# Moving the denominator sums of two token tiles by one FFN group in a fused attention and FFN kernel

## The chip, the cores and the metric

The kernel runs on one core of one Trainium2 chip. The metric is device time in microseconds (us) of one execution. The time given for a kernel is the median of several executions. The profile shows one further execution, taken by the hardware profiler.

In this text PE is the matrix engine, PEld its weight loads, DVE the vector engine, ACT the scalar engine, POOL the GpSimd engine, and SP the engine that issues nearly all transfers of this kernel. Every engine works through its own instructions in the order in which they were written.

## The reference

The input has 2048 tokens of 512 features in bf16. Two branches are computed from the same `A_x` rows and mixed by a gate for each token. (Branch B is called with `x`, the rows of branch A.)

```python
qkv = x @ wqkv                       # 32 heads of 16 features
phi = lambda t: where(t > 0, t + 1, exp(t)) + 1e-6
pq, pk = phi(q), phi(k)
kv  = einsum("bhsd,bhse->bhde", pk, v)
z   = einsum("bhsd->bhd", pk)
num = einsum("bhqd,bhde->bhqe", pq, kv)
den = einsum("bhqd,bhd->bhq", pq, z)[..., None] + 1e-6
a   = merge_heads(num / den) @ wo

b   = (silu(x @ w1) * (x @ w3)) @ w2  # hidden width 1376
g   = sigmoid((x * gate_w).sum(-1))
out = g * a + (1 - g) * b
```

## The kernel before

The 2048 tokens are 16 tiles of 128 tokens, and 4 blocks of 4 tiles. The hidden width of 1376 is ten groups of 128 and a remainder of 96 features. The schedule is written out by hand: the order of the calls in the source is the order in each engine's queue, and an engine that waits holds up all that is queued behind it.

The first stage, to about 47 us, projects q and k for all tiles, applies `phi`, and sums the products of keys and tokens in four PSUM banks. Then come the four blocks. In each, `glu_step(tb, fc)` is called for the ten groups (fc = 0 to 9): four matmuls for the gate (line 264), four for the up projection (line 270), a Silu on ACT (line 275) and a product on DVE (line 276) that writes one slice of `hT`. After the groups, `out_step(tb, tt)` is called for the four tiles: four matmuls of the attention branch (line 430, which read `pqT` and `M2`), a scaling on ACT (line 435), eleven matmuls of the second FFN layer (line 443, ten over the groups and one over the remainder), the mix on DVE (line 447), and the store (line 460).

Two helpers stand between these steps.

`den_step(t)` makes the scaled queries of tile t. `den_sums` does three instructions on DVE: a sum over the 16 features of each head (line 287), an addition of 1e-6 (line 290), and a reciprocal (line 294). `den_products(t + 1)` then puts one product on POOL for the next tile (line 283, tile `pr`), and `den_scale(t)` one scaling on POOL (line 298, tile `pqs`) and one transposing transfer on SP's queue (line 303, into `pqT`). The POOL queue therefore holds the product of tile t + 1 ahead of the scaling of tile t.

`rem_step(tb)` computes the remainder of the hidden width and the gates of a block: two times eight matmuls into two banks (line 231), Silu and Tanh on ACT (lines 237 and 238), a product on DVE for each half (line 241, into `hrem`), two small DVE instructions that finish the gates (lines 246 and 250), and one transposing transfer on SP's queue (line 254, from `hrem` into the last slice of `hT`).

The banks are handed out in turn. `mm_tile` gives banks 4 to 7 one after the other; gate, up and both remainder halves each take one:

```python
def mm_tile():
    turn["mm"] += 1
    return bank[4 + (turn["mm"] - 1) % 4]
```

In block 0 the turn falls so: the eighth group (fc = 7) takes banks 5 and 6, the two remainder halves take banks 7 and 4, the ninth group (fc = 8) takes 5 and 6, and the tenth (fc = 9) takes 7 and 4. The first matmul of the tenth group waits for the DVE instruction of line 241 that empties bank 7, its fifth for the one that empties bank 4. (In the profile's view of instructions these four banks are called bank_144 to bank_147.)

In block 0 the order of the helpers is fixed by a table, `den_at`, and by the place of the calls inside the loop. Under the same fc the denominator step stands ahead of the remainder step. For blocks 1 to 3 both are called between the `out_step`s of the block before.

Of the kernel before, what the change touches and what calls it, by code (L numbers as in the profile page):

```python
# [16 lines left out]
def kernel(  # L17
# [363 lines left out]
    def z_step():  # L381
        zT = work.tile([P, KC], FP32, tag="zT", bufs=1, name="zT")
        nc.vector.tensor_reduce(out=zT[:], in_=zaT[:], op=ALU.add, axis=AX.X)
        nc.vector.tensor_copy(out=zTb[:], in_=zT[:])
        dq.dma_start(out=zrow[0, :].rearrange("(p kc) -> p kc", kc=KC), in_=zTb[:])
        dq.dma_start(out=zpk[:], in_=zrow[0:1, :].to_broadcast([P, D]))
# [73 lines left out]
            dq.dma_start(out=rows[:, cs], in_=o[:, cs])  # L460

    z_step()
    den_at = {5: 0, 6: 1, 7: 2, 8: 3}
    for tb in range(NTB):
        for fc in range(FC):
            glu_step(tb, fc)
# [49 lines left out]
```

## Time and profile before

| | before |
|---|---|
| median of 3 runs | 181.23 us (181.0 to 181.37) |
| profiled execution: time, span | 180.97 us, 179.3 us |
| PE busy | 173.4 us, 97% of the span |
| DVE busy | 101.7 us, 57% |
| ACT busy | 62.6 us, 35% |
| POOL busy | 62.8 us, 35% |
| granted PE clock | 1.0 throughout |

The profiled execution's own time is 1.67 us above its span, which is what lies around the instructions that the profile shows. The chain of work that ended last is followed backwards from the last instruction. Each step goes to what released it, or to the instruction before it on the same engine. PE carries 93% of that chain and DVE 4%. A matmul instruction overlaps the next one, so the distance between the starts of two rows says how fast PE advances, and not the length of a row.

### The profile page before, as it was taken

How to read it: one execution, taken by the hardware profiler on the slowest of the kernel's cores; microseconds unless marked ns; L12 is line 12 of the kernel's file. 1: busy time of each engine (PE TensorE's matmuls, PEld its weight loads, DVE VectorE, ACT ScalarE, POOL GpSimd, SP SyncE). 2: the span in 40 equal slices, each digit the busy share in tenths (PEclk: the TensorE clock that was granted, in tenths of full speed). 3: DMA queues.
4: the chain of work that ended last, by engine and by line, in shares of the span. 5: the costliest groups of instructions: out<-in, count | busy, mean ns of one | idle time of the engine just before them, and what ended most of it. 6: DMA issues, size and time to landing. Idle time of an engine off the chain costs nothing.

```text
span 179.3 us, 2489 instructions
## 1 busy us (share of the span) xinstructions
PE 173.4 (97%) x863; PEld 84.1 (47%) x879; DVE 101.7 (57%) x196; ACT 62.6 (35%) x114; POOL 62.8 (35%) x104
## 2 busy tenths in 40 slices
PE   8999999999999979999999999999999999999993
PEld 5444444444454544644444454444445544444452
DVE  1299789888775896566343256644335564333222
ACT  3354543544736332222323222232321323332130
POOL 5077657656300877445400044540004432000000
PEclk9999999999999999999999999999999999999999
DMA  5988959992103022233200003420000332000011
GB/s 171 269 206 238 168 103 331 386 349 80 33 0 29 0 59 59 62 88 88 59 0 4 0 29 88 91 59 4 0 0 29 88 91 59 0 0 0 29 37 54
DMA packets 29724, 15.41 MB, mean 86 GB/s; under 512 B 21552, under 2 KB 28048, under 8 KB 29712
## 3 DMA queue, kind: packets, MB, share of 16 engines
q1 hardware_dynamic: 29440, 15.25, 33.8%
q8 instruction: 7, 0.11, 0.3%
q10 hardware_dynamic: 272, 0.01, 0.1%
q14 instruction: 5, 0.04, 0.1%
HBM read 8.56 MB, written 2.10 MB: 59 GB/s over the span
## 4 chain that ended last, share of the span: by engine, by line
PE 93%; DVE 4%; issue 1%; DVEq 0%
PE bank L443 21%; PE bank L264 18%; PE bank L270 17%; PE bank L169 16%; PE bank L217 8%; PE bank L430 8%; PE bank L231 2%; PE bank L317 2%; DVE den L290 1%; DVE hT L276 1%; DVE den L287 1%; PE bank L405 0%; PE bank L418 0%; PE bank L323 0%; DVE o L447 0%
## 5 line engine op out<-in xcount | busy, mean ns | idle before, releaser
L276 DVE TENSOR_TENSOR hT<-bank,sg 128x512 bf16<-128x512 f32 x40 | 27.2, 681 | 31.6 <-PE bank L270 28.5
L264 PE MATMUL bank<-xT,w 128*128 128x512 bf16 x158 | 40.9, 379 | 1.4 <-DVE hrem L241 1.2
L443 PE MATMUL bank<-w,hT 128*128 128x512 bf16 (+4 forms) x197 | 40.6, 355 | 0.1
L275 ACT ACTIVATE sg<-bank 128x512 bf16<-128x512 f32 x40 | 23.9, 597 | 47.6 <-PE bank L264 46.5
L270 PE MATMUL bank<-xT,w 128*128 128x512 bf16 x154 | 40.3, 379 | 0.2
L298 POOL TENSOR_TENSOR pqs<-pq,rden 128x512 bf16<-128x512 bf16 x16 | 16.9, 1055 | 56.1 <-issue 50.8
L169 PE MATMUL bank<-wqk,xT 128*128 128x512 bf16 x126 | 30.8, 386 | 0.1
L447 DVE SCALAR_TENSOR_TENSOR o<-bank,omg_all,aga 128x512 bf16<-128x512 f32 (+2 forms) x18 | 12.4, 692 | 27.5 <-PE bank L443 27.4
L443 PEld LDWEIGHTS <-hT 128*128 128x128 bf16 (+1 forms) x198 | 18.5, 98 | 20.0 <-DMA hT<-hrem 0.2
L201 POOL TENSOR_TENSOR zacc<-zacc,pk 128x128 f32<-128x128 f32 x56 | 23.3, 445 | 10.4 <-DVE pk L187 10.4
L264 PEld LDWEIGHTS <-w 128*128 128x128 bf16 x160 | 15.6, 98 | 19.7 <-issue 1.4
L270 PEld LDWEIGHTS <-w 128*128 128x128 bf16 x160 | 15.7, 98 | 18.9
L283 POOL TENSOR_TENSOR pr<-pq,zb 128x512 f32<-128x512 bf16 x16 | 18.4, 1153 | 11.7 <-ACT zb L389 11.7
L435 ACT ACTIVATE aga<-bank,g_all 128x512 f32<-128x512 f32 x16 | 11.0, 687 | 28.9 <-PE bank L430 27.8
L169 PEld LDWEIGHTS <-xT 128*128 128x128 bf16 x128 | 12.6, 99 | 15.1 <-issue 0.5
L217 PE MATMUL bank<-pk,xN 128*128 128x512 bf16 x62 | 16.3, 379 | 0.2
L430 PE MATMUL bank<-M,pqT 128*128 128x512 bf16 x61 | 16.3, 378 | 0.2
L182 ACT ACTIVATE eq<-bank 128x512 bf16<-128x512 f32 x16 | 9.4, 597 | 16.0 <-PE bank L169 14.9
L187 DVE SCALAR_TENSOR_TENSOR pk<-bank,emk 128x512 bf16<-128x512 f32 x16 | 11.1, 692 | 1.6
L182 ACT ACTIVATE ek<-bank 128x512 bf16<-128x512 f32 x16 | 9.4, 597 | 7.1 <-PE bank L169 7.1
L187 DVE SCALAR_TENSOR_TENSOR pq<-bank,emq 128x512 bf16<-128x512 f32 x16 | 11.1, 692 | 0.6
L287 DVE TENSOR_REDUCE den<-pr 128x32 f32<-128x512 f32 x16 | 10.8, 676 | 0.0
(49 smaller groups left out, 82.9 us busy)
## 6 DMA issues: line engine op xcount, KB each, us to landing
w<-in_B_w_dram SPq DMA_DIRECT2D x3, 1280.0 KB, 10.6
out_dram<-o SPq DMA_DIRECT2D x15, 128.0 KB, 1.9
wqk<-in_A_wqkv_dram SPq DMA_DIRECT2D x4, 256.0 KB, 4.0
xN<-in_A_x_dram SPq DMA_DIRECT2D x1, 1024.0 KB, 5.8
xN<-in_A_x_dram SPq DMA_DIRECT2D x2, 256.0 KB, 3.0
xN<-in_A_x_dram SPq DMA_DIRECT2D x1, 512.0 KB, 3.7
wv<-in_A_wqkv_dram SPq DMA_DIRECT2D x1, 512.0 KB, 11.6
wo<-in_A_wo_dram SPq DMA_DIRECT2D x1, 512.0 KB, 12.5
```

What stands on the lines that cost most here:

```text
L169: nc.tensor.matmul(ps[:], lhsT=xT[:, kc, t * P : (t + 1) * P], rhs=w[:, kc, :], start=(kc == 0), stop=(kc == KC - 1),)
L182: nc.scalar.activation(out=e[:], in_=ps[:], func=ACT.Exp)
L187: nc.vector.scalar_tensor_tensor(out=dst, in0=ps[:], scalar=0.0, in1=em[:], op0=ALU.max, op1=ALU.add)
L201: nc.gpsimd.tensor_tensor(out=(zaccb if t == NT - 1 else zacc)[:, cs], in0=zacc[:, cs], in1=pk[t][:, cs], op=ALU.add,)
L217: nc.tensor.matmul(bank[kc][:], lhsT=xN[:, t, kc * P : (kc + 1) * P], rhs=pk[t][:], start=(t == 0), stop=(t == NT - 1),)
L264: nc.tensor.matmul(g_ps[:], lhsT=w1[:, kc, fs], rhs=xT[:, kc, tok], start=(kc == 0), stop=(kc == KC - 1),)
L270: nc.tensor.matmul(u_ps[:], lhsT=w3[:, kc, fs], rhs=xT[:, kc, tok], start=(kc == 0), stop=(kc == KC - 1),)
L275: nc.scalar.activation(out=sg[:], in_=g_ps[:], func=ACT.Silu)
L276: nc.vector.tensor_tensor(out=hT[tb][:, fc, :], in0=u_ps[:], in1=sg[:], op=ALU.mult)
L283: nc.gpsimd.tensor_tensor(out=pr[t][:], in0=pq[:, t, :], in1=zb[:], op=ALU.mult)
L430: nc.tensor.matmul(a_ps[:], lhsT=pqT[:, c, ts], rhs=M2[:, c, :], start=(c == 0), stop=(c == KC - 1),)
L443: nc.tensor.matmul(b_ps[:, 0:w], lhsT=hT[tb][:n, fc, tl], rhs=w2[:n, fc, cs], start=(fc == 0), stop=(fc == FC),)
```

## The change

In block 0 the denominator steps of the third and fourth tile (tiles 2 and 3) are called one group later each. Nothing else in the source changes.

```diff
     z_step()
-    den_at = {5: 0, 6: 1, 7: 2, 8: 3}
+    den_at = {5: 0, 6: 1, 8: 2, 9: 3}
     for tb in range(NTB):
         for fc in range(FC):
             glu_step(tb, fc)
             if tb == 0:
                 if fc in den_at:
                     den_step(den_at[fc])
...
                 if fc == 7:
                     rem_step(0)
```

The orders on PE, ACT and POOL are the same in both kernels. On DVE the three sums of tile 2 go from ahead of the two products of line 241 to behind the `hT` product of the ninth group; the three sums of tile 3 go from ahead of the `hT` product of the tenth group to behind it, ahead of the first line 447. On SP the transfer of line 254 and the line 303 transfer of tile 2 change places.

## The prediction

> **What bounds the kernel now.** I read the page's busy shares first (PE 97%), then the list of waits, to see what the other 3% holds. It has only one wait of PE for another engine after the start:
>
> ```profile
> PE bank L264 <- DVE hrem L241: 1.2, 1, 1.2
> ```
>
> The columns are engine, tile and line, what it waited for, total us, times, longest. The timeline of PE around that wait gives its place (start, us, engine, line; idle time in brackets):
>
> ```profile
> 63.63 1.03 PE L264 MATMUL bank<-xT,w 128*128 128x512 bf16 x3
> 64.50 1.03 PE L270 MATMUL bank<-xT,w 128*128 128x512 bf16 x4
> 66.68 1.02 PE L264 MATMUL bank<-xT,w 128*128 128x512 bf16 x4 [1.16 <-DVE hrem L241]
> 67.54 1.03 PE L270 MATMUL bank<-xT,w 128*128 128x512 bf16 x4
> 68.40 1.03 PE L430 MATMUL bank<-M,pqT 128*128 128x512 bf16 x4
> 69.27 2.54 PE L443 MATMUL bank<-w,hT 128*128 128x512 bf16 x11
> ```
>
> These are the ninth group, the tenth, and the start of the first out_step. Groups of four matmuls start 0.86 to 0.87 us apart when nothing waits. The tenth group should have started at 64.50 + 0.87 = 65.37 and started at 66.68, so the stop costs 1.31 us of PE's pace (the 1.16 in brackets is measured from the modelled end).
>
> The timeline of DVE in the same stretch says why line 241 came late:
>
> ```profile
> 63.66 0.63 DVE L276 TENSOR_TENSOR hT<-bank,sg 128x512 bf16<-128x512 f32 x1
> 64.21 0.67 DVE L287 TENSOR_REDUCE den<-pr 128x32 f32<-128x512 f32 x1
> 64.92 1.11 DVE L290 TENSOR_SCALAR den<-den 128x32 f32<-128x32 f32 x1
> 66.06 0.35 DVE L294 RECIPROCAL rden<-den 128x32 f32<-128x32 f32 x1
> 66.33 0.56 DVE L241 TENSOR_TENSOR hrem<-bank,sgr 128x192 bf16<-128x192 f32 x2
> 66.81 0.77 DVE L246 TENSOR_SCALAR g_all<-th_all 128x4 f32<-128x4 f32 x1
> 67.49 0.16 DVE L250 TENSOR_SCALAR omg_all<-th_all 128x4 f32<-128x4 f32 x1
> 67.56 0.68 DVE L276 TENSOR_TENSOR hT<-bank,sg 128x512 bf16<-128x512 f32 x1
> ```
>
> The three sums of tile 2 (64.21 to 66.33) stand ahead of line 241. One of them, the small addition of line 290, took 1.11 us where its median is 0.18. The timeline of POOL shows its company:
>
> ```profile
> 63.83 1.05 POOL L298 TENSOR_TENSOR pqs<-pq,rden 128x512 bf16<-128x512 bf16 x1 [0.51 <-DVE rden L294]
> 64.84 1.15 POOL L283 TENSOR_TENSOR pr<-pq,zb 128x512 f32<-128x512 bf16 x1
> 66.50 1.05 POOL L298 TENSOR_TENSOR pqs<-pq,rden 128x512 bf16<-128x512 bf16 x1 [0.51 <-DVE rden L294]
> 67.51 1.15 POOL L283 TENSOR_TENSOR pr<-pq,zb 128x512 f32<-128x512 bf16 x1
> ```
>
> Line 290 ends at 66.03, POOL's product at 65.99; line 246 (0.77 instead of 0.16) ends at 67.58, POOL's scaling at 67.55. Small additions on DVE end when the POOL instruction beside them ends. The chain that ended last runs over PE from 66.68 to the last mix at 176.33, with no wait for another engine. So 1.31 us taken from this stop should shorten the whole, if nothing else becomes late.
>
> **Part 1: line 241 no longer behind the sums of tile 2.** With those gone from its front, the first line 241 starts at 64.21, where the reduction started. Its inputs are there: ACT's Silu and Tanh of the halves end by 63.56 and 64.23. Before, PE restarted 0.35 us after the first line 241 began (66.33 to 66.68); now bank 7 is free for PE at 64.56, 0.81 us ahead of need. The second starts about 0.24 later and ends by about 64.8; bank 4 is needed at 65.37 + 0.86 = 66.23. PE therefore does not stop: minus 1.31 us. Could line 241 itself be held by POOL, which scales tile 1 from 63.83 to 64.88 and then makes a product to 65.99? Before, the second line 241 ran from about 66.57 with POOL busy from 66.50, and both were over in 0.56, so by the nearest row no. The other end is that it waits until 65.99: PE restarts at 66.34 and the gain is 66.68 - 66.34 = 0.34. I take the first, as it is the same instruction beside the same POOL work.
>
> **Part 2: lines 246 and 250.** They come up at 64.69 (two line 241s took 0.48 to the next start). By the row at 66.81, line 246 ends with the running POOL instruction although POOL has the next one ready: about 64.91, then line 250, DVE free about 65.0. The ninth group's hT product cannot start before PE ends at 65.53 plus the usual 0.11 (86.32 to 86.43 in block 1): 65.64. If line 246 is instead held through POOL's next product, it ends near 66.03 and the product starts at 66.17. Either way that product, at 67.56 before, is earlier.
>
> The Trainium skill, "SBUF — State Buffer", section "Who interferes with whom", says that a tensor_scalar may use the port pair that DVE shares with GpSimd, and that whoever issues first holds it for the whole instruction. It speaks against this change in so far as the blocked addition does not vanish but moves. On its words alone line 246 might lose again to the next POOL instruction; then the later end above holds, and the total is still the same. The long lines 290 and 246 agree with it.
>
> **Part 3: the sums of tile 2 behind the ninth hT product.** hT 65.64 to 66.33; reduction from about 66.25; line 290 at 66.96 with POOL idle (its product for tile 3 ended at 65.99, its scaling of tile 2 waits for these sums), so 0.18; reciprocal at 67.18 to 67.53. The tenth hT product is next at 67.45; PE finishes its operand at 66.23 + 1.03 = 67.26, so the sums hold it up by only 0.1. It ends at 68.08, or 68.6 with part 2's later end. The second-layer matmuls of the first out_step start at 67.96 (69.27 less 1.31) and advance 0.216 each (2.38 for eleven), so they reach the tenth slice at 69.90. Spare: 1.8, at worst 1.3. Cost nothing; beyond that spare each us costs one.
>
> **Part 4: the sums of tile 3 behind the tenth hT product.** Reduction at 68.00; line 290 at 68.71. POOL's scaling of tile 2 starts at 67.61 (0.08 after the reciprocal, as at 63.83) and the product of tile 4 runs about 68.62 to 69.77, so line 290 pays the long price of 1.11 here: +0.93 on what it was. The reciprocal ends at 70.20. Behind it waits the first mix (line 447), which PE releases at 67.96 + 2.54 = 70.50 plus 0.11. Hidden, with 0.4 to spare; and its bank is wanted again only at the third out_step's line 443, near 75.8. Line 290 of tile 4 then comes at 71.99 while POOL works until 72.44 and may lose 0.3; the next mix is not released before 73.85.
>
> **Part 5: POOL and SP.** POOL's order stands. The scaling of tile 2 goes from 66.50 to 67.61, that of tile 3 from 69.57 to 70.28. Each issues one transpose on SP (1.19 on the queue, 2.4 to landing). Line 254 now stands ahead of tile 2's transpose: its data is complete at 64.8, the transpose of tile 1 holds SP from 64.91 to 66.10, so it issues at 66.1 and lands at 68.5; the remainder's matmul needs it at 67.96 + 10 x 0.216 = 70.12. Before it was issued at 68.86 and the weight load waited 0.24 for it, hidden. Tile 2's transpose issues at 68.7, lands 71.1, and is needed by the third out_step at 76.22 - 1.31 = 74.9; tile 3's lands near 73.8 and is needed near 78.2. Tile 0's, unmoved, lands at 62.24 + 2.4 = 64.6 and is now needed at 67.10. The first store is issued after tile 3's transpose, 71.36 + 1.19 = 72.6, as before (72.70). All cost nothing.
>
> **The sum.** 180.97 - 1.31 = 179.66 for the profiled execution. That execution was 0.26 below the median of the runs; on the median, 181.23 - 1.31 = 179.92. I predict 179.9. Such a kernel's measurement can tell about 0.2%, or 0.36 us, from no change.
>
> **The rivals.** *Line 241 blocked by POOL*, or DVE otherwise late by 1.2 to 1.5 us: the gain shrinks to 0.34 and the time is 180.9, which counts as no change. Against it stands the unblocked line 241 at 66.33; for it, that POOL works there without a gap to 65.99. Chance 0.06. *The stop was not line 241's*, and the tenth group waits for something else that frees at 66.6: 181.2. Against it: DVE's next instructions in time are those of line 241, and PE starts 0.35 after the first. Chance 0.03. *Slower: tile 2's transpose becomes the wait.* It is issued 68.7 instead of 67.58 and wanted 1.31 earlier. If it landed after 10.4 us, as the large weight loads did, it would arrive at 79.1, PE would wait 79.1 - 74.9 = 4.2, and the time would be 179.9 + 4.2 = 184.1. It decides from a landing at 74.9, and the whole is slower by 0.2% from 74.9 + 1.31 + 0.36 = 76.6. Against it: the neighbouring transposes landed in 2.4 each. Chance 0.04. A lesser PE wait of some tenths inside the first out_steps, from part 3 or 4, is the rest of my doubt about the size, not the sign.
>
> **The numbers.** Full removal 0.87 (faster). The run spread (-0.23, +0.14 about the median), a new wait of up to 0.6 and the pace's last 0.05 give 179.5 to 180.5. Part of it stays at 180.9 or 181.2 in 0.09, slower in 0.04. Faster by over 0.2%: 0.88, with a little of the first rival; same 0.08; slower 0.04.
>
> **What would show it.** In the changed profile: no idle PE before the tenth group's line 264, which starts near 65.4; line 241 near 64.2; line 290 of tile 2 at 0.18 and of tile 3 near 1.1; line 254 issued near 66.1; the last mix near 175.0 and a span near 178.0. It would be wrong if line 241 stretched beside POOL, or if a wait of line 430 or 443 for pqT or hT appeared.

## The result, and the profile after

The changed kernel takes 179.75 us (median of 7 runs, 179.1 to 180.43), against 181.0 for the kernel before in 7 runs. The ratio is 0.9921, with a 95% interval of 0.9895 to 0.9946: 1.4 us less, between 1.0 and 1.9 (the two medians differ by 1.25). Its profiled execution took 179.95 us, with a span of 178.2.

The waits of PE in the profile after are down to one line, which lies at the program's start. The wait for line 241 is gone.

```profile
PE bank L317 <- PEq L500: 0.8, 1, 0.8
```

The timeline of PE after, the same groups as shown of before (start, us, engine, line):

```profile
64.78 1.03 PE L270 MATMUL bank<-xT,w 128*128 128x512 bf16 x4
65.64 1.03 PE L264 MATMUL bank<-xT,w 128*128 128x512 bf16 x4
66.50 1.03 PE L270 MATMUL bank<-xT,w 128*128 128x512 bf16 x4
67.37 1.03 PE L430 MATMUL bank<-M,pqT 128*128 128x512 bf16 x4
68.23 2.54 PE L443 MATMUL bank<-w,hT 128*128 128x512 bf16 x11
```

The tenth group's line 264 starts 0.86 after the line 270 ahead of it, where it was 2.18 before. No row has a bracket with idle time. This profile runs 0.28 later than the one before on reaching the ninth group (64.78 against 64.50), which has nothing to do with the change: the first transposes (line 323) and projections (line 169) at the program's start took longer, and the lag is 0.27 already where line 169 starts at 10.53 against 10.26. So I measure each profile from the start of the ninth group's line 270 to the start of the last mix (line 447). Before, that is 176.33 - 64.50 = 111.83; after, 175.30 - 64.78 = 110.52. The difference is 1.31.

The timeline of DVE after:

```profile
64.48 0.61 DVE L241 TENSOR_TENSOR hrem<-bank,sgr 128x192 bf16<-128x192 f32 x2
65.01 0.17 DVE L246 TENSOR_SCALAR g_all<-th_all 128x4 f32<-128x4 f32 x1
65.09 0.16 DVE L250 TENSOR_SCALAR omg_all<-th_all 128x4 f32<-128x4 f32 x1
65.91 0.69 DVE L276 TENSOR_TENSOR hT<-bank,sg 128x512 bf16<-128x512 f32 x1 [0.66 <-PE bank L270]
66.52 0.68 DVE L287 TENSOR_REDUCE den<-pr 128x32 f32<-128x512 f32 x1
67.23 0.18 DVE L290 TENSOR_SCALAR den<-den 128x32 f32<-128x32 f32 x1
67.44 0.35 DVE L294 RECIPROCAL rden<-den 128x32 f32<-128x32 f32 x1
67.72 0.63 DVE L276 TENSOR_TENSOR hT<-bank,sg 128x512 bf16<-128x512 f32 x1
68.26 0.67 DVE L287 TENSOR_REDUCE den<-pr 128x32 f32<-128x512 f32 x1
68.97 1.11 DVE L290 TENSOR_SCALAR den<-den 128x32 f32<-128x32 f32 x1
70.12 0.35 DVE L294 RECIPROCAL rden<-den 128x32 f32<-128x32 f32 x1
70.89 0.75 DVE L447 SCALAR_TENSOR_TENSOR o<-bank,omg_all,aga 128x512 bf16<-128x512 f32 x1 [0.42 <-PE bank L443]
```

Line 241 starts 2.13 earlier (64.48 - 0.28 = 64.20 against 66.33), line 290 of tile 2 takes its short 0.18, and the long 1.11 has moved to tile 3. After it and the reciprocal DVE still waits 0.42 for the first mix. The timeline of POOL after shows why the two trade lengths: POOL idles 1.61 ahead of the scaling of tile 2, through line 290 of that tile, and the product at 68.89 starts just ahead of line 290 of tile 3.

```profile
64.10 1.05 POOL L298 TENSOR_TENSOR pqs<-pq,rden 128x512 bf16<-128x512 bf16 x1 [0.51 <-DVE rden L294]
65.11 1.15 POOL L283 TENSOR_TENSOR pr<-pq,zb 128x512 f32<-128x512 bf16 x1
67.88 1.05 POOL L298 TENSOR_TENSOR pqs<-pq,rden 128x512 bf16<-128x512 bf16 x1 [1.61 <-DVE rden L294]
68.89 1.15 POOL L283 TENSOR_TENSOR pr<-pq,zb 128x512 f32<-128x512 bf16 x1
```

### The profile page after: what moved, and what is told of

Its sections match the earlier page's. It is cut to its first block, busy times and chain, and to the rows that moved or that the text cites. A ratio compares the mean times of both kernels' runs of the same rounds, so it can differ in the third digit from the quotient of the medians.

```text
span 178.2 us, 2489 instructions
## 1 busy us (share of the span) xinstructions
PE 173.6 (97%) x863; PEld 84.2 (47%) x879; DVE 101.6 (57%) x196; ACT 62.6 (35%) x114; POOL 62.8 (35%) x104
## 4 chain that ended last, share of the span: by engine, by line
PE 97%; issue 1%; DVE 0%
PE bank L443 21%; PE bank L264 20%; PE bank L270 19%; PE bank L169 16%; PE bank L217 8%; PE bank L430 8%; PE bank L231 3%; PE bank L317 2%; PE bank L323 1%; PE bank L405 1%; PE bank L418 0%; DVE o L447 0%
## 5 line engine op out<-in xcount | busy, mean ns | idle before, releaser
L201 POOL TENSOR_TENSOR zacc<-zacc,pk 128x128 f32<-128x128 f32 x56 | 23.3, 445 | 10.4 <-DVE pk L187 10.4
```

The costliest lines, as they stand in the source:

```text
L201: nc.gpsimd.tensor_tensor(out=(zaccb if t == NT - 1 else zacc)[:, cs], in0=zacc[:, cs], in1=pk[t][:, cs], op=ALU.add,)
```

## The experiments

The theory: PE stops because line 241 stands behind the sums of tile 2 on DVE, and those are long because line 290 waits for POOL. Its rivals: the sums of tile 3 carry part of the gain; the bank alone holds PE; DVE is simply too full there; line 290 is long for its own reasons. All kernels start from the kernel before. The stage is the stretch from the ninth group's line 270 to the last mix, worked out as above from the one profile that there is of each kernel. The times of whole runs are compared with runs of the kernel before on the same chip, and carry the scatter of the start: the ninth group's line 270 began anywhere from 63.89 to 64.93 in the profiles of this study. The profiled executions of the three kernels with a stage of 110.52 show it: they took 179.33, 179.58 and 179.95 us with that line at 64.16, 64.42 and 64.78.

| kernel | stage, us | against before | ratio of times, 95% interval |
|---|---|---|---|
| before | 111.83 | | |
| the change | 110.52 | -1.31 | 0.9921 (0.9895 to 0.9946) |
| remainder step first | 110.52 | -1.31 | 0.9924 (0.9902 to 0.9947) |
| tile 3 only | 111.83 | 0.00 | 1.0007 (0.9987 to 1.0027) |
| no addition for tile 2 | 111.22 | -0.61 | 0.9986 (0.9971 to 1.0001) |
| own banks | 111.76 | -0.07 | 0.9999 (0.9979 to 1.0018) |
| own banks, transfer first | 110.67 | -1.16 | 0.9932 (0.9911 to 0.9954) |
| both ahead | 113.86 | +2.03 | 1.0125 (1.0089 to 1.0162) |
| both behind the ninth | 110.52 | -1.31 | 0.9909 (0.9888 to 0.993) |
| both in the out stage | 111.80 | -0.03 | 0.9996 (0.9981 to 1.0011) |
| POOL scales first | 110.90 | -0.93 | 0.9953 (0.9935 to 0.997) |

**Remainder step first.** Tile 3 and the table stay; two calls trade places.

```diff
             if tb == 0:
+                if fc == 7:
+                    rem_step(0)
                 if fc in den_at:
                     den_step(den_at[fc])
...
-                if fc == 7:
-                    rem_step(0)
```

> Table of before; only the remainder step is called ahead of the denominator step of tile 2, within the same group, so on DVE line 241 passes the sums of tile 2, and on SP line 254 passes tile 2's transpose; tile 3 stays where it was. Theory (PE stops because line 241 stands behind the sums of tile 2): no stop of PE at the tenth group, 1.3 us less than before, 179.6 to 179.9. Rival (the gain needs the sums of tile 3 moved too, or the later place of the sums): the tenth hT product comes late and PE waits at the tenth slice; by my count this product ends at 69.65 and is wanted at 69.90, so a wait of a few tenths at most and 180.0 to 180.3.

The timeline of PE at the tenth group:

```profile
64.42 1.03 PE L270 MATMUL bank<-xT,w 128*128 128x512 bf16 x4
65.28 1.03 PE L264 MATMUL bank<-xT,w 128*128 128x512 bf16 x4
```

The whole 1.31 is there, with tile 3 unmoved. The tenth hT product starts at 68.92 and ends at 69.55 in this profile, and no row of PE shows a wait at the tenth slice. The two starts lie 0.86 apart: PE does not stop ahead of the tenth group. So it is enough that the remainder step goes ahead of tile 2's sums, on DVE and on SP. The additions of line 290 still wait for POOL there (0.43 for tile 2, 1.11 for tile 3), and it costs nothing.

**Tile 3 only.**

```diff
-    den_at = {5: 0, 6: 1, 7: 2, 8: 3}
+    den_at = {5: 0, 6: 1, 7: 2, 9: 3}
```

> Only the sums of tile 3 are moved behind the tenth group; tile 2 as before. Theory: the stop of 1.2 us at line 264 stays, the time is that of before, 181.0. Rival (the sums of tile 3, between the ninth and tenth hT products, cost something by themselves): 180.0 to 180.7.

The stage is that of before to 0.01, and the list of waits has the stop again:

```profile
PE bank L264 <- DVE hrem L241: 1.2, 1, 1.2
```

By itself, the half of the change that moves tile 3 is worth nothing.

**No addition for tile 2.**

```diff
-        nc.vector.tensor_scalar(
-            out=den[:], in0=den[:], scalar1=1e-6, scalar2=None, op0=ALU.add
-        )
+        if t != 2:
+            nc.vector.tensor_scalar(
+                out=den[:], in0=den[:], scalar1=1e-6, scalar2=None, op0=ALU.add)
```

> Order of before; the addition of 1e-6 (line 290) is left out for tile 2 only, which takes out the one instruction that ended with POOL's product at 66.0. Theory: line 241 starts at 65.2 instead of 66.3, PE's stop at the tenth group shrinks from 1.3 to about 0.2; but line 254 still stands behind tile 2's transpose on SP, which issues at 67.0, so the remainder slice of hT lands near 70.8 where PE wants it at 70.3: a new wait of about 0.5. Sum: 0.6 us less than before, 180.4. If line 254 is no limit: 1.1 less, 179.9. Rival (the length of line 290 is not POOL's doing and the next instruction takes it over): no change, 181.0.

The timeline of PE shows both parts of the sum, the small stop that is left and the new one:

```profile
64.15 1.03 PE L270 MATMUL bank<-xT,w 128*128 128x512 bf16 x4
65.19 1.02 PE L264 MATMUL bank<-xT,w 128*128 128x512 bf16 x4
...
67.78 2.32 PE L443 MATMUL bank<-w,hT 128*128 128x512 bf16 x10
70.45 0.39 PE L443 MATMUL bank<-w,hT 96*128 96x512 bf16 x1 [0.36 <-DMA hT<-hrem]
```

The tenth group starts 0.17 late (65.19 against 64.15 + 0.87), and the remainder's matmul 0.51 late (70.45 against 67.78 + 10 x 0.216). Together 0.68 of the 1.31 stay, and the stage gives 0.61. The runs' times show only 0.25 less, between 0.5 less and nothing; the 0.6 expected lies just outside, and I cannot say from these runs what makes up the rest.

**Own banks.** The remainder halves of block 0 take two banks that lie idle there.

```diff
-            ps = mm_tile()[:].rearrange("p (j n) -> p j n", j=2)
+            ps = (ab_tile if tb == 0 else mm_tile)()[:].rearrange("p (j n) -> p j n", j=2)
```

> Order of before on DVE, POOL and SP; the remainder step of block 0 takes two banks of the other turn, which lie idle there, so the tenth group no longer waits for line 241. Theory: PE does not stop at the tenth group, but line 241 and with it line 254 are as late as before (issue near 68.9), so the first out_step stops before its last matmul, for the remainder slice, until 71.4: the 1.3 us come back as a wait of PE for that transfer, and the time is 180.9 to 181.1. Rival (the bank is the whole cost): 179.7. It tells whether the bank alone, or the bank and the transfer behind the sums, held PE.

The bank's wait is gone and the time is not. The list of waits has a new one of PE in its place:

```profile
PE bank L443 <- DMA hT<-hrem: 0.9, 1, 0.9
```

The timeline of PE gives its place:

```profile
68.39 2.48 PE L443 MATMUL bank<-w,hT 128*128 128x512 bf16 x10
71.78 0.39 PE L443 MATMUL bank<-w,hT 96*128 96x512 bf16 x1 [0.91 <-DMA hT<-hrem]
```

PE came to the first out_step without a stop and then stood before the last of its matmuls, 71.78 against 68.39 + 2.16 = 70.55. The sums of tile 2 held PE by two ways: the bank, and the remainder's transfer. The second stood just behind the first; in the profile before it shows only as the 0.24 for which the weight load waited.

**Own banks, transfer first.** As above, and on SP line 254 passes tile 2's transpose; DVE's order is that of before.

```diff
-        dq.dma_start(out=pqT[:, :, t * P : (t + 1) * P], in_=pqs[:], transpose=True)
+        if t == 2:
+            held.append(pqs)
+        else:
+            dq.dma_start(out=pqT[:, :, t * P : (t + 1) * P], in_=pqs[:], transpose=True)
...
                 if fc == 7:
                     rem_step(0)
+                    dq.dma_start(out=pqT[:, :, 2 * P : 3 * P], in_=held[0][:], transpose=True)
```

> As the kernel with own banks for the remainder halves of block 0, and on SP line 254 is issued ahead of tile 2's transpose; on DVE the sums of tile 2 still stand ahead of line 241. Theory (the sums of tile 2 hold PE by two ways, the bank and the remainder transfer, and with both cut their place costs nothing): the remainder slice lands near 69.5 on the clock of before, ahead of its need at 70.1, and what is left is a wait of 0.1 to 0.2 for the tenth hT product. From the ninth group's line 270 to the last mix 1.1 to 1.2 us less than before. Rival (DVE itself is the limit, and its work must come later on): no change against before.

With both ways cut, DVE's old order costs 0.15. What is left is a wait of 0.5 of the weight loads for the tenth hT product, most of it covered by the matmuls under way:

```profile
70.36 0.11 PEld L446 LDWEIGHTS <-hT 128*128 128x128 bf16 x2 [0.47 <-DVE hT L276]
```

DVE was not too full; its work stood in the wrong place.

**Both ahead.**

```diff
-    den_at = {5: 0, 6: 1, 7: 2, 8: 3}
+    den_at = {5: (0,), 6: (1,), 7: (2, 3)}
...
-                if fc in den_at:
-                    den_step(den_at[fc])
+                for t in den_at.get(fc, ()):
+                    den_step(t)
```

> The opposite direction: the denominator steps of tiles 2 and 3 both ahead of the remainder step. Theory: line 241 starts at 67.9 on the clock of before instead of 66.3, PE stops 1.5 longer at the tenth group; line 254 now stands behind the transposes of tiles 2 and 3, lands near 73.5 and adds 0.4 to 0.5. Sum: 2.0 us more than before. Rival (only tile 2 matters): no change.

The dose the other way: 2.03 us more, where 2.0 was expected, and both waits in one list, the bank and the transfer.

```profile
PE bank L264 <- DVE hrem L241: 2.7, 1, 2.7
...
PE bank L443 <- DMA hT<-hrem: 0.3, 1, 0.3
```

**Both behind the ninth.** The same code as in the kernel with both ahead, with this table:

```diff
-    den_at = {5: 0, 6: 1, 7: 2, 8: 3}
+    den_at = {5: (0,), 6: (1,), 8: (2, 3)}
```

> Both denominator steps behind the ninth group, ahead of the tenth hT product. Theory: no stop at the tenth group; the tenth hT product starts at 69.3 and ends at 69.9 on the clock of the changed kernel, just when its weight load is due (69.96); this uses up the spare that the prediction gave it. From the ninth group's line 270 to the last mix 1.2 to 1.3 us less than before, as the changed kernel or 0.1 more. Rival (the spare is smaller than worked out, since the second line 290 waits for the next POOL instruction too): a wait at the tenth slice of up to 1.1 and little gain.

The tenth hT product started at 68.66 in this profile, 4.50 after the ninth group's line 270 (at 64.16), as expected, and no wait of PE appears. It ended at 69.29, 0.05 ahead of its weight load (67.40 + 9 x 0.216 = 69.34). The spare of part 3 is real, and this uses all of it. In the changed kernel the same product ended at 68.35 and its weight load came at 68.02 + 9 x 0.216 = 69.96: moving tile 3 as well buys a spare of 1.6, and no time.

**Both in the out stage.**

```diff
-    den_at = {5: 0, 6: 1, 7: 2, 8: 3}
+    den_at = {5: 0, 6: 1}
...
+                if tb == 0 and tt == 0:
+                    den_step(2)
+                    den_step(3)
                 if tt == 1:
                     rem_step(tb + 1)
```

> Both denominator steps after the first out_step: the slower rival of the prediction made to happen. Theory: no stop at the tenth group, but the transpose of tile 2 is issued near 74.0 on the clock of the changed kernel, its data is there 2.5 later, and the third out_step's line 430, due at 75.2, stops for about 1.3. So from the ninth group's line 270 to the last mix about the same as before. Rival (the transposes have more room than worked out): as the changed kernel, 1.3 us less.

This is the prediction's slower rival, forced by a late issue in place of a slow landing. The transpose of tile 2 is issued at 74.00, and the third out_step stops for it:

```profile
76.48 1.04 PE L430 MATMUL bank<-M,pqT 128*128 128x512 bf16 x4 [1.11 <-DMA pqT<-pqs]
```

It gives back 1.28 of the 1.31, so the mechanism exists, but here the sums start 5.0 us later than the change puts them (line 287 of tile 2 at 71.56, against 66.52 on nearly the same clock).

**POOL scales first.** DVE and SP keep the order of before; on POOL the scaling of tile 2 goes ahead of the product of tile 3.

```diff
         den_sums(t)
+        if t == 2:
+            den_scale(t)
         if t + 1 < NT:
             den_products(t + 1)
-        den_scale(t)
+        if t != 2: den_scale(t)
```

> Order of before on DVE and SP; only on POOL the scaling of tile 2 goes ahead of the product of tile 3, so that POOL is idle while DVE does line 290 of tile 2. Theory (line 290 was long because that product ran beside it): line 290 takes 0.18 there, line 241 starts 0.93 earlier, PE's stop shrinks from 1.31 to about 0.38, and the remainder slice, issued near 67.9 on the clock of before, still comes in time. From the ninth group's line 270 to the last mix 0.9 us less than before, 180.0 if before is 180.9. Rival (line 290 is long for another reason, or line 246 or the tenth hT product takes over the wait): no change to 0.3 less.

The timeline of DVE of this kernel:

```profile
64.90 0.18 DVE L290 TENSOR_SCALAR den<-den 128x32 f32<-128x32 f32 x1
65.12 0.35 DVE L294 RECIPROCAL rden<-den 128x32 f32<-128x32 f32 x1
65.39 0.56 DVE L241 TENSOR_TENSOR hrem<-bank,sgr 128x192 bf16<-128x192 f32 x2
```

The timeline of POOL:

```profile
63.81 1.06 POOL L298 TENSOR_TENSOR pqs<-pq,rden 128x512 bf16<-128x512 bf16 x1 [0.50 <-DVE rden L294]
65.55 1.06 POOL L298 TENSOR_TENSOR pqs<-pq,rden 128x512 bf16<-128x512 bf16 x1 [0.68 <-DVE rden L294]
```

And the timeline of PE at the tenth group:

```profile
65.74 1.02 PE L264 MATMUL bank<-xT,w 128*128 128x512 bf16 x4 [0.22 <-DVE hrem L241]
```

With POOL idle from 64.87 to 65.55, line 290 takes 0.18, line 241 follows 0.94 earlier than before, and PE's stop falls by 0.93. So of the 1.31 us, 0.93 was line 290 waiting for POOL. The other 0.38 is what the sums cost without that wait, since they still stand ahead of line 241.

## Why the prediction was right

**The stop.** 1.31 was worked out from PE's pace, and the stage is 1.31 shorter. The whole runs give 1.0 to 1.9, and the median, 179.75, is 0.17 below the 179.92 forecast. That distance is mostly the base: the forecast started from 181.23, the median of three runs, and seven runs give 181.0, from which 1.31 less is 179.69. The span, 178.2, is 0.2 above the 178.0 forecast: that is the late start of 0.28, which the prediction did not carry as a term.

**Part 1.** Line 241 was to start at 64.21; taken from the ninth group it started at 64.48 - 0.28 = 64.20. POOL scaled beside it, and it took 0.61 for the two. The first rival, line 241 blocked by POOL, did not occur in any kernel of this study.

**Part 2.** Line 246 was to end with POOL's scaling at about 64.91. It ended at 65.18, 64.90 on the clock of before, 0.03 after that scaling (65.15). It came up so late in the scaling that this cost it 0.01 at most (0.17 against 0.16), and POOL's next product, recorded from 65.11, held neither it nor line 250.

**Parts 3 and 4.** Line 290 of tile 2 fell to 0.18 and that of tile 3 rose to 1.11, as worked out; the reciprocal ended at 70.47, 0.42 ahead of the first mix. The spare of part 3 was counted to the tenth slice's matmul; its weight load comes 0.21 earlier (68.02 against 68.23 for the first slice), so the spare is 1.6 and not 1.8. The Trainium skill, "SBUF — State Buffer", section "Who interferes with whom", says that a tensor_scalar can, in some of its modes, use the port pair shared with GpSimd and that the later of the two then blocks. The waits agree with it, though no run shows the ports themselves: in the profiles before and after and in the nine experiments line 290 took 0.18 with POOL idle, and beside a POOL instruction it ended 0.02 to 0.04 after that one's end. The objection that the prediction drew from it, that the wait moves and does not vanish, was right for this change, and is why the place matters: the same 1.11 costs 0.93 in front of line 241 and nothing in front of the first mix. Line 290 of tile 4 lost 0.36 (0.54 against 0.18) where 0.3 was allowed, also hidden.

**Part 5.** Line 254 was issued at 66.46, 66.18 on the clock of before, where 66.1 was forecast; the transposes of tiles 2 and 3 followed from 68.96 (68.68, forecast 68.7), and none was waited for. One landing was forecast wrong: tile 2's transpose landed 3.8 after its issue and not 2.4, at 72.5 on the clock of before where 71.1 was forecast. That was still 2.4 ahead of its need at 74.9. The prediction held that the neighbouring transposes landed in 2.4 each and passed over tile 3's, which took 4.1 in the profile before; what makes one of them slower no run here shows. The prediction called the remainder's transfer hidden, and it is so because the change moves line 254 too. With own banks, line 254 behind tile 2's transpose was issued at 69.30 and PE stopped for it, and the gain was 0.07; ahead of that transpose (own banks, transfer first) it was issued at 67.25 and the gain was 1.16.

**The rivals.** That the stop was not line 241's falls with the kernel that only puts the remainder step first, and with POOL's order alone. The slower rival was forced and priced: the wait for tile 2's transpose came at a landing 1.3 after need and gave 1.28 back. The landing of 10.4 that the prediction gave it did not occur; the slowest transpose of `pqT` in this study took 4.3 (in the kernel with own banks).

## What to carry to other kernels

Where the busiest engine has one stop, price it by that engine's pace, and then follow everything that the late instruction releases. Here it released a bank and a transfer, and cutting the first alone gained nothing, since the second arrived at the same time. When work is moved out of the way, ask what stands in front of it in its new place: sums that cost 1.31 ahead of one instruction cost nothing 2.0 us later. A small instruction whose length varies may hold a wait: look which other engine's instruction ends with it.

## What the runs showed of the hardware

A small DVE addition that waits for POOL need not wait for the next POOL instruction in the queue. With both sums behind the ninth group, line 290 of tile 3 came up during a scaling and ended at 68.36, when that ended at 68.33, though POOL's next product started at 68.28. The timeline of DVE and that of POOL:

```profile
67.77 0.59 DVE L290 TENSOR_SCALAR den<-den 128x32 f32<-128x32 f32 x1
```

```profile
67.27 1.06 POOL L298 TENSOR_TENSOR pqs<-pq,rden 128x512 bf16<-128x512 bf16 x1 [1.60 <-DVE rden L294]
68.28 1.15 POOL L283 TENSOR_TENSOR pr<-pq,zb 128x512 f32<-128x512 bf16 x1
```

Line 290 took 1.11 beside a product that started just before it, and 0.59 beside a scaling already half done. The addition right behind such a one can go either way. Line 250, which follows line 246, took 0.16 in the profile before (start 67.49, POOL's product from 67.51). In the kernel with both in the out stage it took 1.19 (start 78.17, POOL's product from 78.19) and ended at 79.36, when that product ended at 79.34. These starts stand alike, and no run shows what decides. The product of line 241 and the reductions of line 287 never showed such a wait: 0.56 to 0.61 for a pair and 0.63 to 0.69, with POOL busy or idle.
